# A one-element exponential ahead of the first exponential that follows each run of Gelus

## The chip, the cores and the metric

The kernel runs on one core of a Trainium2 chip. The metric is device time in microseconds of one execution, lower is better; several executions are timed and the median counts. The engines of the core are TensorE (PE, with its weight loads as PEld), VectorE (DVE), ScalarE (ACT), GpSimd (POOL) and SyncE (SP, which issues transfers). Each engine works through its own instructions in order and waits on semaphores for the others.

## The reference

Two layers, each an attention with a compressive memory and then a GeGLU feed-forward, on 2048 tokens of width 512 in bfloat16. The attention works on four segments of 512 tokens, 32 heads of 16.

```python
def _A_ref(x, wq, wk, wv, wo, beta):
    ...
    for s in range(N):
        ...
        logits = jnp.einsum('bhqd,bhkd->bhqk', qs, ks) * scale + mask
        p = _softmax(logits, axis=-1)
        a_dot = jnp.einsum('bhqk,bhkd->bhqd', p, vs)
        pq = phi(qs)
        num = jnp.einsum('bhld,bhde->bhle', pq, M)
        ...
        pk = phi(ks)
        M = M + jnp.einsum('bhld,bhle->bhde', pk, vs)
        z = z + jnp.einsum('bhld->bhd', pk)
    ...

def _B_ref(x, w_gate, w_up, w_down):
    return _gelu(x @ w_gate) * (x @ w_up) @ w_down

x = A_x
x = x + _A_ref(_layernorm(x, axis=-1), A_wq, A_wk, A_wv, A_wo, A_beta)
x = x + _B_ref(_layernorm(x, axis=-1), B_w_gate, B_w_up, B_w_down)
x = x + _A_ref(_layernorm(x, axis=-1), A_wq, A_wk, A_wv, A_wo, A_beta)
x = x + _B_ref(_layernorm(x, axis=-1), B_w_gate, B_w_up, B_w_down)
```

Here phi(t) is t + 1 for positive t and exp(t) elsewhere. So ACT computes two kinds of function that matter below: Exp (softmax and phi) and Gelu (feed-forward).

## The kernel before

The whole input, all weights and the activations stay on the chip. The work is cut into eight attention blocks (two layers by four segments, numbered k = 0 to 7) and eight feed-forward blocks of the same numbering. A block of scores (token S) fills four of the eight PSUM banks, each of 128 x 512 float32, and an exponential (tokens e for half of them, E for all four) reads them, scales, and writes bfloat16 into a slot of the tile pt. The next block of scores that uses the same banks has to wait until the exponentials have read them. Masks on POOL (or DVE), products with the values on PE, and transposes on DVE follow.

A feed-forward block computes 14 tiles of gate (G) and up (P) products. The gate either is copied to gel_sb first and gets its Gelu there (copy g, then l), or its Gelu is taken straight from PSUM (L). DVE then multiplies by the up product (p). All Gelus of a block stand together on ACT, so that its instructions go from Exp to Gelu and back.

What sets the order is one long string of tokens, ORDER, written out by hand: a loop in `run` reads token by token and emits the instructions of each, and each engine keeps that order. A token's first letters choose the routine, a letter v, s or g behind them the engine (DVE, ACT, POOL), and numbers the block, tile, bank and so on. The attention of later segments is interleaved with the feed-forward of earlier ones, so scores of the next block come right behind the Gelus.

ACT can hold the table of Exp or that of Gelu. The build puts an ACT_TABLE_LOAD ahead of each activation that needs the other one; the load carries line numbers of that activation, and takes over waits that were the activation's. Copies on ACT (ACT.Copy) bring no load with them. There are 14 loads in all: one at the start, seven to Gelu (line 753) and six back to Exp: five ahead of an exponential of scores (line 598, in `exponential`) and one ahead of an exponential for phi (line 655, in `phi_exp`). After the last two feed-forward blocks no exponential follows.

The lines that the prediction names: 481 and 483 are the two forms of a dense product on PE (in four column groups, or whole), 593 the scores, 631 the products with the values, 608 the mask on POOL, 638 a transpose on DVE of those products, 753 the Gelu, 819 the multiplication by the up product, 490 and 492 copies out of PSUM on ACT and DVE, 496 layer-norm statistics, 742 a memset of `constant_column`, 454 and 455 two small exponentials of beta at the start.

Of the kernel before, what the change touches and what calls it, by code (L numbers as in the profile page):

```python
# [9 lines left out]
ACT = mybir.ActivationFunctionType  # L10
ALU = mybir.AluOpType
ENG = mybir.EngineType
F32 = mybir.dt.float32
# [9 lines left out]
L = 512  # L23
# [271 lines left out]
def run(nc, cst, seg, wrk, psp, A_x, A_wq, A_wk, A_wv, A_wo, A_beta, B_x, B_w_gate, B_w_up, B_w_down, out):  # L295
# [86 lines left out]
    def vaug(k):  # L382
        return vaugs[(k - 1) % SETS if k else SETS]
# [90 lines left out]
    def ps(*name):  # L474
        return ps_all[:, bank[name], :]
# [81 lines left out]
    def dense(code, k, b, h, n, bk, columns):  # L557
        name = (code, k, b, h)
        if name not in done:
            done[name], bank[name] = 0, bk  # L560
        pairs, group = ops_of(code, k, b, h)
        for _ in range(n):
            i = done[name]
            done[name] += 1
            size = group or len(pairs)
            if group:
                dst = ps(*name)[:, half * (i // group):half * (i // group) + half]
            elif code == "W":
                c0, c1 = down_columns(h)
                dst = ps(*name)[:, 0:c1 - c0]  # L570
            else:
                dst = ps(*name)
            l, r = pairs[i]
            product(dst, l(), r(), columns, i % size == 0, i % size == size - 1)
# [5 lines left out]
    def score(k, v, b0, b1, s):  # L580
        a_q, a_kf, a_kx = q[k], kf[k], kx[k]
        banks = (b0, b0 + 1, b1, b1 + 1)
        slot[k, v] = s
        bank["S", k, v] = (b0, b1)
        for r in range(2):
            for b, par, ki, q0, n, c0 in ROUNDS_OF[2 * v + r][0]:
                for j in range(4):
                    rows = slice(32 * j, 32 * j + 32 if 1 in par else 32 * j + 16)
                    if 1 in par:
                        lhsT = a_kx[rows, b, ki, 0:P] if 0 in par else a_kx[rows, b, ki, C:3 * C]  # L590
                    else:
                        lhsT = a_kf[rows, b, P * ki:P * ki + P]
                    multiply(ps_all[:, banks[j], UNIT * r + c0:UNIT * r + c0 + n], lhsT=lhsT, rhs=a_q[rows, b, q0:q0 + n],  # L593
                             start=True, stop=True, tile_position=(32 * j, 0))

    def exponential(k, v, p, n):
        s, b0 = slot[k, v], bank["S", k, v][p]
        nc.scalar.activation(out=pt_all[:, s:s + 2, 2 * p:2 * p + 2 * n, :].rearrange("p r h c -> p h r c"),  # L598
                             in_=ps_all[:, b0:b0 + 2 * n, :].rearrange("p h (r c) -> p h r c", r=2), func=ACT.Exp, scale=SCALE)
# [19 lines left out]
    def values(k, u, bk):  # L619
        b, par = u // 2, u % 2  # L620
        bank["F", k, u] = bk
        work = []
        for i in range(*USED[par]):
            t = ROUNDS * b + i
            for _, par2, ki, q0, n, o in ROUNDS_OF[t][0]:
                work.append((t, vz if len(par2) > 1 else vaug(k), ki, q0, n, o))
        work.sort(key=lambda w: w[1] is vz)
        for m, (t, va, ki, q0, n, o) in enumerate(work):
            for j in range(4):
                g = (DH + 1) * (par * H // 2 + 4 * b + j)  # L630
                multiply(ps("F", k, u)[32 * j:32 * j + 32, q0:q0 + n], lhsT=va[:, ki * VW + g:ki * VW + g + 32],  # L631
                         rhs=pt_all[:, slot_of(k, t), j, o:o + n], start=(m == 0), stop=(m == len(work) - 1),
                         tile_position=(0, 32 * j))
# [115 lines left out]
            load(part(vz, slice(C * a, C * a + C), a), part(vaug(k), slice(0, C), a))  # L749


    def gelu(dst, src):
        nc.scalar.activation(out=dst, in_=src, func=ACT.Gelu_apprx_tanh)  # L753

# [7 lines left out]
    def turn_tile(m, j, n, bk):  # L762
        name = ("T", m, j)
        if name not in done:
            done[name], bank[name] = 0, bk
        for _ in range(n):
            kt = done[name]
            done[name] += 1
            turn_by_pe(turned(name)[:, kt, :], xn_of[m, j][:, kt * P:(kt + 1) * P], ident[:])  # L769
# [7 lines left out]

    engine = {"v": nc.vector, "s": nc.scalar, "g": nc.gpsimd}

    for token in ORDER:  # L780
        code, *arg = token.split("/")
        eng = engine.get(arg[0])
        if eng is not None:
            arg = arg[1:]
        i = [int(a) for a in arg]
        k, b = (i + [0, 0])[:2]
        if code in ("Q", "K", "V", "O", "G", "P", "QH", "KH", "GH", "W"):
            dense(code, *i)
        elif code == "S":
            score(*i)  # L790
        elif code == "F":
            values(*i)
        elif code in ("D", "N", "U"):
            memory_product(code, *i)
        elif code == "T":
            turn_tile(*i)
        elif code == "e":
            exponential(k, b, i[2], 1)
        elif code == "E":
            exponential(k, b, 0, 2)  # L800
        elif code == "M":
            mask(eng, k, b)
        elif code in ("q", "k"):
            copy(eng, set_of(k)["qk".index(code)][:, b, :], ps(code.upper(), k, b, 0))
        elif code in ("qh", "kh"):
            cols = slice(half * i[2], half * i[2] + half)
            copy(eng, set_of(k)["qk".index(code[0])][:, b:b + 2, cols], folded((code.upper(), k, b, i[2])))
        elif code == "v":
            copy(eng, by_head(vaug(k))[:, b, :, :, 0:DH], ps("V", k, b, 0).rearrange("p (h a e) -> p h a e", a=2, e=DH))
        elif code == "g":  # L810
            copy(eng, gel_sb[:, b, :], ps("G", k, b, 0))
        elif code == "gh":
            copy(eng, gel_sb[:, 2 * b:2 * b + 2, half * i[2]:half * i[2] + half], folded(("GH", k, b, i[2])))
        elif code == "l":
            gelu(gel_sb[:, b, :], gel_sb[:, b, :])
        elif code == "L":
            gelu(gel_sb[:, b, :], ps("G", k, b, 0))
        elif code == "p":
            nc.vector.tensor_tensor(out=gel_sb[:, b, :], in0=gel_sb[:, b, :], in1=ps("P", k, b, 0), op=ALU.mult)  # L819
        elif code == "w":  # L820
            c0, c1 = down_columns(i[2])
            add_to_x(k, b, c0, c1, ps("W", k, b, i[2])[:, 0:c1 - c0])
        elif code == "o":
            add_to_x(k, b, 0, D, ps("O", k, b, 0))
        elif code == "s":
            c0, c1 = down_columns(i[2])
            load(of[:, tile_of(k) + b, c0:c1], x_sb[:, tile_of(k) + b, c0:c1])
        elif code == "m":
            masked(eng, k, b)
        elif code == "z":  # L830
            values_shared(k)
        elif code == "f":
            value_turn(k, b)
        elif code == "r":
            value_scale(k, b)
        elif code == "b":
            value_back(k, b)
        elif code == "a":
            add_up(eng, k, b)
        elif code == "x":  # L840
            phi_exp(*i)
        elif code == "n":
            e = e_of[i[0], i[1], i[2]]
            eng.tensor_scalar(out=e[:], in0=e[:], scalar1=1.0, scalar2=None, op0=ALU.min)  # L844
        elif code == "y":
            phi_sum(*i)
        elif code == "t":
            phi_turn(k, b)
        elif code == "d":
            inverse(k)  # L850
        elif code == "am":
            scaled(*i)
        elif code == "tm":
            scaled_turn(k, b)
        elif code == "ua":
            add_sums(k)
        elif code == "ub":
            spread(k)
        elif code == "st":
            stats(k, b)  # L860
        elif code == "sc":
            scales(k, b)
        elif code == "xn":
            xn_of[k, b] = normed(eng, k, b, i[2])
        elif code == "xt":
            nc.sync.dma_start_transpose(out=part_of_x(k, b), in_=xn_of[k, b][:])
        elif code == "tc":
            copy(eng, part_of_x(k, b), turned(("T", k, b)))
        elif code == "c":
            constant_column(k)  # L870
        elif code == "X":
            load_x(k)
        elif code == "Zo":
            load(w_att["o"][:, k, :], w_view(A_wo)[:, k, :])
        elif code == "Zg":
            ffn_columns(wg_sb, B_w_gate, k)
        elif code == "Zu":
            ffn_columns(wu_sb, B_w_up, k)
        else:
            down_rows(slice(2 * k, 2 * k + 2))  # L880
# [55 lines left out]
```

## Time and profile before

| what | value |
|---|---|
| median of the runs | 540.68 us (540.21, 540.68 and 1830.87) |
| profiled execution, own time | 542.1 us |
| its span in the profile | 540.2 us |
| ACT busy | 423.3 us (78%), 503 instructions |
| DVE busy | 442.1 us (82%) |
| POOL busy | 275.6 us (51%) |
| granted clock of TensorE | full in all 40 slices of the span |

The span runs from the first to the last instruction that the profile holds, and the rest of an execution's time lies around it. Busy time of PE is given in the prediction; matmuls overlap in its pipeline, so the ends of matmuls are modelled. A row of the timeline gives start, duration, engine, line, operation, operands, how many instructions are merged, and, in brackets, the idle time of that engine ahead of the row and who ended it.

### The profile page before, as it was taken

Reading aid. Unit: us, or ns where it says so; the run is one execution under the profiler, and the core shown is the slowest. Engines: PE = TensorE matmul, PEld = TensorE weight load, DVE = VectorE, ACT = ScalarE, POOL = GpSimd, SP = SyncE. Lnnn points to the kernel's source line nnn. Section 1 sums busy time; section 2 is a strip of 40 time slices with the busy share of each in tenths; the row PEclk is TensorE's granted clock in tenths of the full one; section 3 lists DMA queues with packets and bytes.
Section 4 is the critical chain, followed back from the end, with each engine's and each line's share of the span. In section 5 each row is a group of like instructions: output and inputs, shape, how many; then the busy total and the mean of one; then the engine's idle time right before and its main releaser. Section 6 shows DMA issues by size and latency. Waiting matters only on the chain.

```text
span 540.2 us, 21100 instructions
## 1 busy us (share of the span) xinstructions
PE 521.6 (97%) x9255; PEld 276.9 (51%) x9321; DVE 442.1 (82%) x864; ACT 423.3 (78%) x503; POOL 275.6 (51%) x356
## 2 busy tenths in 40 slices
PE   7989999999999999999999999999999999999997
PEld 4444467455654455544554444454555456545444
DVE  7988998899899988899887888978888886776543
ACT  6989998998999778887889888887799867830430
POOL 4798764267658787578752545641544036501000
PEclk9999999999999999999999999999999999999999
DMA  8594143213002133230432130312031005200001
GB/s 276 132 183 88 36 74 124 60 32 65 9 16 46 24 61 46 39 42 11 63 51 54 29 51 4 62 24 30 4 81 24 2 2 81 63 1 0 21 0 59
DMA packets 69134, 27.98 MB, mean 52 GB/s; under 512 B 53426, under 2 KB 69042, under 8 KB 69042
## 3 DMA queue, kind: packets, MB, share of 16 engines
q1 hardware_dynamic: 68752, 26.36, 24.1%
q8 instruction: 73, 1.20, 0.9%
q10 hardware_dynamic: 290, 0.26, 0.2%
q14 instruction: 19, 0.16, 0.1%
HBM read 9.70 MB, written 2.10 MB: 22 GB/s over the span
## 4 chain that ended last, share of the span: by engine, by line
PE 86%; DMA 4%; ACT 3%; issue 2%; DVE 2%; SPq 1%; POOL 0%; ACTq 0%; DVEq 0%
PE ps L483 46%; PE ps L481 24%; PE ps L593 8%; PE ps L631 6%; ACT pt L598 2%; DMA x_sb<-in_A_x_dram 2%; DMA xnT<-xn 2%; PE ps L698 1%; SPq L312 1%; DMA wg_sb<-in_B_w_gate_dram 1%; POOL pt L608 0%; DVE byq L638 0%; ACT wd_sb L490 0%; PE ps L769 0%; DVE st L496 0%
## 5 line engine op out<-in xcount | busy, mean ns | idle before, releaser
L598 ACT ACTIVATE pt<-ps 128x1024 bf16<-128x1024 f32 (+1 forms) x231 | 275.3, 1234 | 47.1 <-PE ps L593 33.7
L608 POOL TENSOR_SCALAR_AFFINE_SELECT pt<-pt 128x256 bf16<-128x256 bf16 (+1 forms) x192 | 106.3, 571 | 158.0 <-ACT pt L598 152.1
L819 DVE TENSOR_TENSOR gel_sb<-gel_sb,ps 128x512 bf16<-128x512 bf16 x112 | 72.3, 680 | 22.4 <-PE ps L483 15.4
L483 PE MATMUL ps<-wd_sb,gel_sb 128*128 128x512 bf16 (+1 forms) x335 | 71.6, 351 | 2.2 <-issue 1.9
L483 PE MATMUL ps<-xnT,wu_sb 128*128 128x512 bf16 x279 | 67.4, 379 | 0.9 <-issue 0.5
L483 PE MATMUL ps<-xnT,wg_sb 128*128 128x512 bf16 (+1 forms) x292 | 60.4, 344 | 1.2 <-issue 1.0
L757 DVE TENSOR_TENSOR x_sb<-x_sb,ps 128x512 bf16<-128x512 bf16 (+1 forms) x68 | 43.4, 649 | 19.3 <-PE ps L483 13.1
L638 DVE STREAM_TRANSPOSE byq<-ps 128x512 f32<-128x512 f32 x64 | 45.4, 709 | 10.9 <-PE ps L631 8.4
L481 PE MATMUL ps<-xnT,wg_sb 128*32 128x512 bf16 (+1 forms) x800 | 50.1, 373 | 0.0
L492 DVE CAST gel_sb<-ps 128x512 bf16<-128x512 f32 x61 | 40.9, 679 | 10.3 <-PE ps L483 7.3
L753 ACT ACTIVATE gel_sb<-gel_sb 128x512 bf16<-128x512 bf16 x85 | 47.4, 623 | 0.6 <-DVE gel_sb L492 0.5
L483 PEld LDWEIGHTS <-gel_sb 128*128 128x128 bf16 x353 | 32.2, 98 | 29.7 <-issue 1.5
L753 ACT ACTIVATE gel_sb<-ps 128x512 bf16<-128x512 f32 x27 | 15.7, 592 | 36.5 <-PE ps L483 35.1
L483 PEld LDWEIGHTS <-wu_sb 128*128 128x128 bf16 x288 | 27.5, 98 | 32.2 <-issue 0.4
L496 DVE BATCH_NORM_STATS2 st<-x_sb 128x6 f32<-128x512 bf16 x60 | 40.7, 678 | 0.5 <-DMA x_sb<-in_A_x_dram 0.2
L481 PE MATMUL ps<-xnT,wu_sb 128*32 128x512 bf16 x640 | 39.8, 379 | 0.6 <-ACT pt L598 0.6
L483 PEld LDWEIGHTS <-wg_sb 128*128 128x128 bf16 x304 | 27.8, 98 | 23.7 <-issue 2.0
L678 POOL TENSOR_SCALAR kx<-kf,masks 128x256 bf16<-128x256 bf16 (+1 forms) x30 | 38.6, 1299 | 0.9 <-PE ps L593 0.7
L616 POOL TENSOR_SCALAR_AFFINE_SELECT pt<-pt 64x1024 bf16<-64x1024 bf16 x26 | 31.0, 1191 | 12.6 <-ACT pt L598 11.7
L844 POOL TENSOR_SCALAR e<-e 128x512 bf16<-128x512 bf16 x21 | 31.7, 1512 | 6.9 <-ACT e L655 6.3
L631 PE MATMUL ps<-pt,vaug 128*32 128x256 bf16 (+2 forms) x1344 | 34.8, 238 | 0.2 <-POOL pt L608 0.2
L481 PE MATMUL ps<-wd_sb,gel_sb 128*32 128x512 bf16 (+1 forms) x604 | 34.8, 364 | 0.0
(138 smaller groups left out, 863.6 us busy)
## 6 DMA issues: line engine op xcount, KB each, us to landing
vz<-vaug SPq DMA_DIRECT2D x14, 136.0 KB, 2.6
wu_sb<-in_B_w_up_dram SPq DMA_DIRECT2D x8, 224.0 KB, 3.9
wg_sb<-in_B_w_gate_dram SPq DMA_DIRECT2D x8, 224.0 KB, 3.8
wd_sb<-in_B_w_down_dram SPq DMA_DIRECT2D x7, 256.0 KB, 4.7
x_sb<-in_A_x_dram SPq DMA_DIRECT2D x3, 512.0 KB, 7.2
out_dram<-x_sb SPq DMA_DIRECT2D x12, 128.0 KB, 1.8
xnT<-xn SPq DMA_TRANSPOSE x48, 2.6
wk_sb<-in_A_wk_dram SPq DMA_DIRECT2D x2, 256.0 KB, 4.5
```

What stands on the lines that cost most here:

```text
L481: multiply(dst[r], lhsT=lhsT[:, r], rhs=rhs, start=start, stop=stop, tile_position=(0, 32 * c))
L483: multiply(dst, lhsT=lhsT, rhs=rhs, start=start, stop=stop)
L492: eng.tensor_copy(out=dst, in_=src)
L496: nc.vector.bn_stats(out=st[:, 0, :], in_=x_sb[:, tile_of(m) + j, :])
L593: multiply(ps_all[:, banks[j], UNIT * r + c0:UNIT * r + c0 + n], lhsT=lhsT, rhs=a_q[rows, b, q0:q0 + n], start=True, stop=True, tile_posit ...
L598: nc.scalar.activation(out=pt_all[:, s:s + 2, 2 * p:2 * p + 2 * n, :].rearrange("p r h c -> p h r c"), in_=ps_all[:, b0:b0 + 2 * n, :].rea ...
L608: nc.gpsimd.affine_select(out=view, in_=view, pattern=[[0, 4], [0, n], [1, C]], compare_op=ALU.is_ge, fill=0.0, base=C, channel_multiplier=-1)
L631: multiply(ps("F", k, u)[32 * j:32 * j + 32, q0:q0 + n], lhsT=va[:, ki * VW + g:ki * VW + g + 32], rhs=pt_all[:, slot_of(k, t), j, o:o + n ...
L638: nc.vector.transpose(out=byq[k, u // 2][:, u % 2, :, :].rearrange("p a c -> p (a c)"), in_=ps("F", k, u))
L753: nc.scalar.activation(out=dst, in_=src, func=ACT.Gelu_apprx_tanh)
L757: nc.vector.tensor_tensor(out=xt, in0=xt, in1=src, op=ALU.add)
L819: nc.vector.tensor_tensor(out=gel_sb[:, b, :], in0=gel_sb[:, b, :], in1=ps("P", k, b, 0), op=ALU.mult)
```

## The change

A tile of two float32 on one partition is set to zero by DVE, ahead of the loop over the tokens. Whenever the loop comes to a token of an exponential (e or E for scores, x for phi) for the first time since a Gelu, it first emits an Exp on ACT of one element of that tile into the other. This happens six times. Nothing reads the result.

```diff
+    idle = cst.tile([1, 2], F32, name="idle")
+    nc.vector.memset(idle[:], 0.0)
+
+    def exponentials_next():
+        nc.scalar.activation(out=idle[:, 1:2], in_=idle[:, 0:1], func=ACT.Exp)
+
     def gelu(dst, src):
         nc.scalar.activation(out=dst, in_=src, func=ACT.Gelu_apprx_tanh)
...
+    gelus = False
     for token in ORDER:
         code, *arg = token.split("/")
+        if gelus and code in ("e", "E", "x"):
+            exponentials_next()
+            gelus = False
+        gelus = gelus or code in ("l", "L")
         eng = engine.get(arg[0])
```

How the instructions stand on ACT at the third of the six places (Gelus of feed-forward block 2, then the scores of attention block 4). gel_sb holds gates, ps is PSUM, pt the exponentials of scores, e an exponential for phi; the names in brackets are the semaphores waited for. Before:

```order
L753 ACTIVATE gel_sb<-ps 128x512
L753 ACTIVATE gel_sb<-gel_sb 128x512 x7
L598 ACT_TABLE_LOAD [waits DVE_49,PE_49]
L598 ACTIVATE pt<-ps 128x2x2x256 [waits Pool_49]
L655 ACTIVATE e<-q 128x512 [waits DMAHW7_49,DMAHW0_49]
L598 ACTIVATE pt<-ps 128x2x2x256 [waits PE_49]
```

And the same place with the change:

```order
L759 ACTIVATE gel_sb<-ps 128x512
L759 ACTIVATE gel_sb<-gel_sb 128x512 x7
L756 ACT_TABLE_LOAD
L756 ACTIVATE idle<-idle 1x1
L598 ACTIVATE pt<-ps 128x2x2x256 [waits DVE_49,PE_49,Pool_49]
L655 ACTIVATE e<-q 128x512 [waits DMAHW7_49,DMAHW0_49]
```

The load now belongs to the new instruction and carries no wait; the waits for DVE and PE went to the exponential. The fifth and sixth places (blocks 4 and 5) read alike. At the first place (block 0) the load of before waited for DVE alone:

```order
-L598 ACT_TABLE_LOAD [waits DVE_49]
-L598 ACTIVATE pt<-ps 128x2x2x256 [waits PE_49] x2
+L759 ACT_TABLE_LOAD
+L759 ACTIVATE gel_sb<-gel_sb 128x512 [waits Activation_49]
+L759 ACTIVATE gel_sb<-gel_sb 128x512 [waits DVE_49]
+L759 ACTIVATE gel_sb<-gel_sb 128x512 x12
+L756 ACT_TABLE_LOAD
+L756 ACTIVATE idle<-idle 1x1
+L598 ACTIVATE pt<-ps 128x2x2x256 [waits DVE_49,PE_49]
+L598 ACTIVATE pt<-ps 128x2x2x256 [waits PE_49]
```

Here too the wait for DVE went over to the exponential; the rows of Gelus only have new line numbers. At the second place the load stood ahead of an exponential for phi and had no wait before either. On DVE one memset of the new tile is added ahead of the first statistics of the token list; PE, POOL and SP keep their instructions and their order.

## The prediction

> **What bounds the kernel now.** I read the busy shares first, then the waits of TensorE (PE), then the groups of ScalarE (ACT), then the stretch of the timeline around each switch of ACT's table from Gelu back to Exp. The page's first part, busy time and share of the span:
>
> ```profile
> PE 521.6 (97%) x9255; PEld 276.9 (51%) x9321; DVE 442.1 (82%) x864; ACT 423.3 (78%) x503; POOL 275.6 (51%) x356
> ```
>
> PE is the bound: 521.6 of 540.2 us, so 18.6 us of idleness is all that a change off PE can take away. What PE waits for, from the table of waits of PE (waiter, awaited, us in total, times, longest):
>
> ```profile
> PE ps L483 <- DMA xnT<-xn: 2.2, 2, 1.3
> PE ps L593 <- ACT pt L598: 1.7, 3, 0.9
> PE ps L481 <- ACT pt L598: 0.6, 1, 0.6
> ```
>
> PE waits for exponentials of scores (line 598) 2.3 us in these two rows, three times and once. The question is whether those four waits lie behind table switches. The groups of ACT (busy us, mean ns, then idle us before them and who ended it):
>
> ```profile
> L598 ACT ACT_TABLE_LOAD x5 | 6.4, 1283 | 5.5 <-PE ps L593 3.7 <-issue 1.3 <-DVE gel_sb L819 0.5
> L655 ACT ACT_TABLE_LOAD x1 | 1.3, 1283 | 0.0
> ```
>
> There are six switches back to Exp, five carried by an exponential of scores and one by an exponential of q. Each load takes 1.283 us, and ACT sat idle 5.5 us ahead of the five: 3.7 for scores of PE, 1.3 listed as issue, 0.5 for VectorE (DVE). In these cases the load stood behind a wait that concerns only the exponential.
>
> Now the six places in the timeline (start us, duration us, engine, line, operation; in brackets the idle time ahead and who ended it). Third switch:
>
> ```profile
> 235.46 0.62 ACT L753 ACTIVATE gel_sb<-gel_sb 128x512 bf16<-128x512 bf16 x1
> 237.85 0.64 PE L593 MATMUL ps<-q,kf 16*128 16x256 bf16 x12
> 238.54 1.28 ACT L598 ACT_TABLE_LOAD   x1 [2.46 <-PE ps L593]
> 239.83 1.02 ACT L598 ACTIVATE pt<-ps 128x1024 bf16<-128x1024 f32 x1
> 240.91 1.69 PE L481 MATMUL ps<-xnT,wu_sb 128*32 128x512 bf16 x28 [0.58 <-ACT pt L598]
> ```
>
> The last Gelu ends at 235.46 + 0.62 = 236.08. ACT then idles 2.46 us until the scores are there, loads 1.28 us, and only then runs the exponential. PE stands still for 0.58 us at 240.33, until that exponential has emptied its banks. Fifth switch:
>
> ```profile
> 369.70 0.60 ACT L753 ACTIVATE gel_sb<-ps 128x512 bf16<-128x512 f32 x1 [0.45 <-PE ps L481]
> 371.09 0.41 PE L593 MATMUL ps<-q,kx 32*128 32x64 bf16 x20
> 371.56 1.28 ACT L598 ACT_TABLE_LOAD   x1 [1.27 <-PE ps L593]
> 372.86 1.94 ACT L598 ACTIVATE pt<-ps 128x1024 bf16<-128x1024 f32 x2
> 373.93 0.20 PE L593 MATMUL ps<-q,kx 32*128 32x64 bf16 x2 [0.17 <-ACT pt L598]
> 374.85 0.40 PE L593 MATMUL ps<-q,kx 32*128 32x64 bf16 x10 [0.71 <-ACT pt L598]
> ```
>
> Gelu ends at 370.30, the scores come 1.27 us later, the load delays both exponentials, and the next scores, which go into the same banks, wait 0.17 + 0.71 = 0.88 us. Sixth switch:
>
> ```profile
> 424.73 2.18 ACT L753 ACTIVATE gel_sb<-gel_sb 128x512 bf16<-128x512 bf16 x4
> 427.70 0.40 PE L593 MATMUL ps<-q,kx 32*128 32x64 bf16 x12
> 428.19 1.28 ACT L598 ACT_TABLE_LOAD   x1 [1.27 <-issue]
> 429.48 1.94 ACT L598 ACTIVATE pt<-ps 128x1024 bf16<-128x1024 f32 x2
> 431.47 0.29 PE L593 MATMUL ps<-q,kx 32*128 32x64 bf16 x8 [0.86 <-ACT pt L598]
> ```
>
> Gelu ends at 426.91 and the load begins at 428.19. The bracket says issue, but by the program's order this load waits for DVE and PE, and the scores end at 427.70 + 0.40 = 428.10, so I read it as the wait for scores. PE then waits 0.86 us. The stalls sum to 0.58 + 0.88 + 0.86 = 2.32 us, the whole 1.7 + 0.6 of the table above: every such wait of PE lies right behind a load.
>
> The other three switches have no stall of PE. First (ahead of it, Gelus without a gap), second and fourth:
>
> ```profile
> 101.88 1.28 ACT L598 ACT_TABLE_LOAD   x1
> 103.17 1.94 ACT L598 ACTIVATE pt<-ps 128x1024 bf16<-128x1024 f32 x2
> 106.11 1.94 ACT L598 ACTIVATE pt<-ps 128x1024 bf16<-128x1024 f32 x2 [0.48 <-POOL pt L608]
> 108.36 0.29 PE L593 MATMUL ps<-q,kf 16*128 16x64 bf16 x8
> ```
>
> ```profile
> 170.81 1.28 ACT L655 ACT_TABLE_LOAD   x1
> 172.64 1.86 ACT L598 ACTIVATE pt<-ps 128x2048 bf16<-128x2048 f32 x1
> 175.69 0.40 PE L593 MATMUL ps<-q,kf 16*128 16x256 bf16 x12
> ```
>
> ```profile
> 294.67 0.60 ACT L490 ACTIVATE kf<-ps 128x512 bf16<-128x512 f32 x1 [0.33 <-PE ps L483]
> 295.72 1.28 ACT L598 ACT_TABLE_LOAD   x1 [0.45 <-DVE gel_sb L819]
> 297.16 1.94 ACT L598 ACTIVATE pt<-ps 128x1024 bf16<-128x1024 f32 x2 [0.15 <-PE ps L593]
> 299.54 0.40 PE L593 MATMUL ps<-q,kf 16*128 16x256 bf16 x12
> ```
>
> At the first two the load starts as soon as ACT is free, so there is nothing to pull forward. At the fourth ACT is free at 295.27 and waits 0.45 us for DVE, yet the exponential waits another 0.15 us for its scores after the load: this load is hidden already. PE has some room behind each. The scores at 108.36 follow the exponentials that end at 108.05 (0.31 us), those at 175.69 the one that ends at 174.50 (1.19), those at 299.54 the ones that end at 299.10 (0.44).
>
> **The change, part by part.** It adds one memset on DVE, six Exp of one element on ACT, and moves six loads from the exponential to the new instruction, which waits for nothing. The other engines issue the same rows in the same order.
>
> The memset stands ahead of the first statistics of the token list. The nearest rows are that statistic and a memset of 8 columns:
>
> ```profile
> 10.59 0.69 DVE L496 BATCH_NORM_STATS2 st<-x_sb 128x6 f32<-128x512 bf16 x1 [0.21 <-DMA x_sb<-in_A_x_dram]
> ...
> 14.15 0.07 DVE L742 MEMSET gel_sb<- 128x8 uint32 x1
> ```
>
> DVE idles 0.21 us there for a transfer of x, so 0.07 us is covered. Without that cover DVE would be 0.07 us late.
>
> The one-element Exp has no row. The nearest is the Exp of 32 elements, the farthest one of 512:
>
> ```profile
> L455 ACT ACTIVATE tmp_e<-ps 128x32 f32<-128x32 f32 x1 | 0.2, 217 | 0.0
> L655 ACT ACTIVATE e<-q 128x512 bf16<-128x512 bf16 x24 | 14.6, 629 | 0.0
> ```
>
> I take 0.21 us, by the row of 32 elements: from 32 to 512 elements it grows by 0.41 us, under 1 ns an element, so 1 element saves almost nothing on it. The ends for the range are 0 (it overlaps the next ACTIVATE wholly) and 0.63.
>
> At the first two switches and the fourth: two of them get 0.21 us later on ACT (0.31 and 1.19 us of room behind them, so PE sees nothing; with 0.63 the first would cost 0.32). At the fourth the load could start at 295.27, the new Exp ends at 295.27 + 1.28 + 0.21 = 296.76, and the scores still decide at 297.16. Nothing gained, nothing lost.
>
> Third switch: the load starts at 236.08, the Exp ends at 237.57, ahead of the scores at 238.54. The exponential starts 1.29 us earlier (239.83 less 238.54), so PE's 0.58 us go. Fifth: load to 371.58, Exp to 371.79. The scores are there at 371.56, so 0.23 us of load and Exp still stick out, and the exponentials start at 371.79 instead of 372.86, 1.07 us earlier: more than the 0.88 us stall. Sixth: 426.91 + 1.28 + 0.21 = 428.40 instead of 429.48, 1.08 us earlier against a stall of 0.86. What decides behind each is then PE's own row of work.
>
> Sum: 0.58 + 0.88 + 0.86 = 2.3 us less. With 0.63 for the new Exp, the fifth and sixth give 0.65 each and the first loses 0.32: 1.6 us less. If the pulled-forward exponentials carried through whole, 1.29 + 1.07 + 1.08 = 3.4 us is the most. The profiled execution took 542.1 us for a span of 540.2, 1.9 outside it; it becomes 539.8. It lies 1.4 us over the median of the runs, 540.68, and I take the difference off that: 540.7 - 2.3 = 538.4.
>
> Here the Trainium skill speaks against the change: ScalarE: Activation LUTs, section What ACT_TABLE_LOAD costs, prices a switch at about 1.28 us of load and 1.38 us of drain, 2.66 us together. This trace has the load's 1.283 us but no drain around it: at the first switch the exponential starts at 103.17, 0.01 us after the load. By the page, with 1.38 us more at each moved switch, the fifth and sixth would come 0.3 us later than now, and the sum would be about 2.2 us more, not 2.3 less. The trace does not bear that out, as far as it shows switches without a wait.
>
> **The rivals.** First, the gain is given back: PE gets there earlier and meets the next thing that isn't ready. For it speaks the longest thing besides PE's own work on the chain that ended last, after the third switch (start us, us, what):
>
> ```profile
> 340.48 0.72 DVE byq L638
> 343.25 4.20 DMA xnT<-xn
> ```
>
> If that chain did not move, the third switch's 0.58 us would be lost there: 1.74 left, 538.9. Against it: the chain starts from products of PE (DVE's transpose reads what PE wrote), so it moves too, and the fifth and sixth switches come later, with no transfer on the chain after 347.5. If all is absorbed, 540.7, no change.
>
> Second, the change doesn't do what it says: the load stays behind a wait, or the exponential waits longest for something else (its third wait, for POOL, that the load did not carry). Then 540.7. Against it: in the new order the load and the Exp carry no wait, and the exponentials after the third, fifth and sixth loads start 0.01 to 0.02 us after the load ends, so POOL was not late by then; whether it was in time 1.1 us earlier these rows do not show.
>
> Third, on the other side: the switch is not over when the load is over, and the new Exp pays for the rest. Its place is ACT between load and first exponential; call its time D. The third switch gains its 0.58 up to D = 1.88; the fifth and sixth gain 1.28 - D each, at most their stalls; the first loses what D exceeds 0.31, the second 1.19, the fourth 1.04 (0.60 of slack ahead of its scores and 0.44 behind). The sum turns at D = 1.1 us. Were D another load's time on top, 1.28 + 0.21 = 1.49, it is -0.58 + 0.42 + 1.18 + 0.30 + 0.45 = 1.8 us more: 542.5. Against it: no row of ACT under 512 elements without a load takes over 0.6 us. Of this kind is the drain of the Trainium skill's page above, and it would give 540.7 + 2.2 = 542.9.
>
> **How the numbers follow.** The sum at work: 0.62, 538.4, by itself 537.3 (3.4 us) to 539.1 (1.6 us). Gain given back in part or whole, 538.9 to 540.7: 0.20. No effect, 540.7: 0.11. Slower by the switch's rest, 542.5: 0.07. Of these, 0.03 go to the rule of the Trainium skill's page on ScalarE, at 542.9. The runs shown differ by 0.5 us (540.21 and 540.68; 1830.87 I leave out as a disturbance), and the profiled one is 1.4 over. So the range goes 0.5 below the most that can be gained, 536.8, and 0.3 above no effect, 541.0; the slower rival and part of the scatter, under 0.2, stay outside. A difference of 2%, 10.8 us, is about what a measurement of this kernel can tell from no change. PE's waits for exponentials are 2.3 us, the one rival that loses loses 2; so within 2% has 0.98, and 0.01 goes to either side for what I haven't seen.
>
> **What would show it.** In the profile of the changed kernel: six loads and six one-element Exp on the new line, of 1.28 and 0.2 us; idle time ahead of the loads gone (5.5 us now) and found ahead of the exponentials, waiting for PE; the three stalls of PE behind the third, fifth and sixth switches gone or under 0.2 us; no new wait of PE at 106 to 109. I am wrong if the new Exp takes more than 0.63 us, if the stalls go and the span doesn't shrink by 1.5 us or more (then the first rival, and the place where PE waits instead must show), or if the exponentials after the loads start no earlier against their scores than before.

## The result, and the profile after

The changed kernel takes 538.0 us (median of 5 runs, 537.55 to 538.56), the kernel before 540.69 in the runs beside it: a ratio of 0.9949, with an interval of 0.9933 to 0.9964. That is 2.7 us less. The profiled execution took 538.0 us for a span of 535.9; the one before had 542.1 and 540.2, so the two profiles differ by 4.1 to 4.3 us, more than the medians; the second run of the kernel before shows below where most of that rest lies. Two executions far outside the others, one of 1830.87 us of the kernel before and one of 666.4 us of the Copy kernel below, are in no ratio.

PE in the first part of the page after (busy us, share of the span, instructions):

```profile
PE 520.5 (97%) x9255; PEld 276.5 (52%) x9321; DVE 441.4 (82%) x865; ACT 424.1 (79%) x509; POOL 275.9 (51%) x356
```

Of the 4.3 us by which the span is shorter, 3.2 are idleness of PE (18.6 us before, 15.4 now). The other 1.1 us are busy time, which rests on modelled ends. The groups of ACT that belong to the new line (busy us, mean ns, then idle us before them):

```profile
L756 ACT ACT_TABLE_LOAD x6 | 7.7, 1283 | 0.1
L756 ACT ACTIVATE idle<-idle 1x1 f32<-1x1 f32 x6 | 1.2, 202 | 0.1
```

All six loads moved to the new line and cost 1.283 us each as before, but ACT idles 0.1 us ahead of them instead of 5.5. The Exp of one element takes 0.202 us. The waits of PE after:

```profile
PE ps L483 <- DMA xnT<-xn: 1.4, 2, 1.0
PE ps L483 <- ACT pt L598: 0.2, 1, 0.2
```

The rows for scores (line 593, 1.7 us) and column-group products (line 481, 0.6 us) that waited for exponentials are gone. Of the waits for exponentials only the 0.2 us at line 483, which were there before, are left. The timeline of the third switch after:

```profile
235.00 1.28 ACT L756 ACT_TABLE_LOAD   x1
236.29 0.20 ACT L756 ACTIVATE idle<-idle 1x1 f32<-1x1 f32 x1
236.76 0.63 PE L593 MATMUL ps<-q,kf 16*128 16x256 bf16 x12
237.45 1.02 ACT L598 ACTIVATE pt<-ps 128x1024 bf16<-128x1024 f32 x1 [0.96 <-PE ps L593]
239.06 1.68 PE L481 MATMUL ps<-xnT,wu_sb 128*32 128x512 bf16 x28
240.67 0.40 PE L593 MATMUL ps<-q,kf 16*128 16x256 bf16 x12
```

Load and Exp stand in the time in which ACT waits anyway; 0.96 us of the wait are left, and they stand ahead of the exponential now. PE's products at 239.06 have no bracket, where they had 0.58 us. Fifth and sixth:

```profile
367.72 0.60 ACT L759 ACTIVATE gel_sb<-ps 128x512 bf16<-128x512 f32 x1 [0.45 <-PE ps L481]
368.34 1.28 ACT L756 ACT_TABLE_LOAD   x1
369.12 0.41 PE L593 MATMUL ps<-q,kx 32*128 32x64 bf16 x20
369.63 0.20 ACT L756 ACTIVATE idle<-idle 1x1 f32<-1x1 f32 x1
369.74 1.90 ACT L598 ACTIVATE pt<-ps 128x1024 bf16<-128x1024 f32 x2
371.72 0.40 PE L593 MATMUL ps<-q,kx 32*128 32x64 bf16 x12
374.54 0.29 PE L593 MATMUL ps<-q,kx 32*128 32x64 bf16 x8
...
423.62 1.28 ACT L756 ACT_TABLE_LOAD   x1
424.40 0.40 PE L593 MATMUL ps<-q,kx 32*128 32x64 bf16 x12
424.73 2.58 PE L481 MATMUL ps<-xnT,wu_sb 128*32 128x512 bf16 x44
425.03 1.90 ACT L598 ACTIVATE pt<-ps 128x1024 bf16<-128x1024 f32 x2
427.24 0.29 PE L593 MATMUL ps<-q,kx 32*128 32x64 bf16 x8
```

At the fifth the scores end at 369.12 + 0.41 = 369.53 and the exponentials start at 369.74, since a piece of load and Exp sticks out. That is early enough: the next scores at 371.72 run in one piece of 12 and without a bracket, where they came in two pieces with 0.17 and 0.71 us of waiting.

To compare kernels without the scatter of whole executions, I use a distance on PE: from the scores that the first exponential after a switch reads to a later block of scores (the next one at the third and sixth switch, the next but one at the fifth). Before it is 242.53 - 237.85 = 4.68 us at the third switch, 377.67 - 371.09 = 6.58 at the fifth and 431.47 - 427.70 = 3.77 at the sixth. After it is 3.91, 5.42 and 2.84. The three switches give 0.77 + 1.16 + 0.93 = 2.86 us. A further 0.11 us goes just behind the third switch, where two products on PE start 0.33 us apart before (243.96 and 244.29) and 0.22 after (242.09 and 242.31), so PE gains about 2.97 us in all. This second step repeats in the other runs with one Exp at that switch and is in none without; no bracket names what PE waits for there.

### The profile page after: what moved, and what is told of

It reads as the page before. It is cut to its first block, busy times and chain, and to the rows that moved or that the text cites. A ratio compares the mean times of both kernels' runs of the same rounds, so it can differ in the third digit from the quotient of the medians.

```text
span 535.9 us, 21107 instructions
## 1 busy us (share of the span) xinstructions
PE 520.5 (97%) x9255; PEld 276.5 (52%) x9321; DVE 441.4 (82%) x865; ACT 424.1 (79%) x509; POOL 275.9 (51%) x356
## 4 chain that ended last, share of the span: by engine, by line
PE 93%; DMA 2%; DVE 2%; issue 1%; ACT 1%; POOL 1%; DVEq 0%; SPq 0%
PE ps L483 50%; PE ps L481 26%; PE ps L593 9%; PE ps L631 7%; DMA xnT<-xn 1%; ACT pt L598 1%; PE ps L698 1%; DMA x_sb<-in_A_x_dram 1%; POOL pt L608 0%; DVE st L402 0%; PE ps L775 0%; DVE byq L638 0%; PE ps L447 0%; DVE xn L391 0%; DVE gel_sb L492 0%
## 5 line engine op out<-in xcount | busy, mean ns | idle before, releaser
L830 DVE TENSOR_TENSOR gel_sb<-gel_sb,ps 128x512 bf16<-128x512 bf16 x112 | 72.2, 679 | 20.3 <-PE ps L483 15.4
```

## The experiments

The theory that I tested (A): the gain is PE's stall behind three of the six loads, and it is as large as the time by which the exponentials come earlier, up to that stall. Its rivals: B, the gain comes from elsewhere (the other three switches, or the memset and the tiles shifted by the new one), and C, it only matters that the load stands ahead of the wait, whatever time the extra instruction takes.

### The three switches with a stall, and the other three

A counter of the switches picks those at which the Exp is emitted.

```diff
-    gelus = False
+    gelus, switch = False, 0
...
         if gelus and code in ("e", "E", "x"):
-            exponentials_next()
+            switch += 1
+            if switch in (3, 5, 6):
+                exponentials_next()
             gelus = False
```

> The one-element Exp at the third, fifth and sixth switch alone. Theory A (the gain is PE's stall behind these three loads, 0.77 + 1.15 + 0.93 = 2.85 us by PE's rows of the two profiles): the whole gain of the change, about 538.0 us, ratio 0.995; on PE, from the scores at a switch to the next scores 3.91 us at the third (4.68 before), from the scores to the next but one at the fifth 5.42 (6.58 before), to the next at the sixth 2.84 (3.77 before). Theory B (the gain comes from the other places, or from the shifted tiles and the memset): part of it or nothing, up to 540.7, and the first 90 us shorter by 0.8 in every variant that has the memset.

Measured: 537.33 us beside 540.52, ratio 0.9932 (0.9915 to 0.9949); distances 3.91, 5.43 and 2.85 us. The whole gain is there: 2.84 us by the distances, and 3.2 by the medians. The other kernel has `(1, 2, 4)` in place of `(3, 5, 6)`.

> The one-element Exp at the first, second and fourth switch alone. Theory A: no gain, 540.7 us, at most 0.2 more, with the three stalls of PE as before (4.68, 6.58 and 3.77 us between the scores). Theory B: a part of the gain stays, 538.0 to 540.0.

Measured: 540.28 us beside 540.52, ratio 0.9990 (0.9979 to 1.0001); distances 4.67, 6.58 and 3.77 us. No gain that can be told from none, and all three stalls are back, at the same size as in the kernel before (its timeline at the third, fifth and sixth switch):

```profile
237.65 1.28 ACT L598 ACT_TABLE_LOAD   x1 [2.46 <-PE ps L593]
240.02 1.69 PE L481 MATMUL ps<-xnT,wu_sb 128*32 128x512 bf16 x28 [0.58 <-ACT pt L598]
...
374.15 0.40 PE L593 MATMUL ps<-q,kx 32*128 32x64 bf16 x10 [0.71 <-ACT pt L598]
...
430.64 0.29 PE L593 MATMUL ps<-q,kx 32*128 32x64 bf16 x8 [0.85 <-ACT pt L598]
```

So the gain sits at the third, fifth and sixth switch, and the other three Exps give nothing.

### An instruction that moves no table

```diff
-        nc.scalar.activation(out=idle[:, 1:2], in_=idle[:, 0:1], func=ACT.Exp)
+        nc.scalar.activation(out=idle[:, 1:2], in_=idle[:, 0:1], func=ACT.Copy)
```

> A one-element Copy in place of the one-element Exp, at all six places: the same memset, tile and number of instructions on ACT, but the load stays with the exponential and its waits. Theory A: no gain, 540.7 us, up to 0.3 more where the Copy has no wait to hide in. Theory B (placement, memset): 538.0.

Measured: 539.87 us beside 540.52, ratio 0.9984 (0.9972 to 0.9996). The loads stay at lines 598 and 655. At the third switch the Copy runs at once, and the load waits behind it for the scores:

```profile
234.03 0.18 ACT L756 ACTIVATE idle<-idle 1x1 f32<-1x1 f32 x1
236.58 1.28 ACT L598 ACT_TABLE_LOAD   x1 [2.37 <-PE ps L593]
```

The distances are those of before: 4.67, 6.57 and 3.77 us. So the three stalls are all there, and the theory holds where it speaks. The time is 0.65 us lower than before all the same, and the interval just leaves out no change. The profile puts no part of that at the switches: at the sixth switch this execution stands 2.30 us ahead of the kernel before, of which 1.41 had come by the scores at 38 us and 0.53 between 203 and 236 us. The next two runs bear on that.

### The kernel before once more, and the memset alone

> The kernel before, unchanged, once more. It shows how far two executions of one program differ, and where. The first stretch is the question: at the scores near 38 us the four variants profiled so far, all with the memset, stand 0.6 to 1.7 us earlier than the kernel before. Theory A (scatter of the first transfers): this profile, too, differs there from the first one by up to 1.5 us, and its time is 540.5, ratio 1.000. Theory B (the memset or the shifted tiles make the start earlier): the start stays where it was, within 0.2 us.

Measured: 540.73 us beside 540.70, ratio 0.9998 (0.9990 to 1.0007). Its profile stands 1.14 us ahead of the first profile of the same program at the scores near 38 us, 0.76 at 237.85 and 0.68 at the sixth switch. The rows of PE at the place where they part, in the first profile (two rows) and in this one:

```profile
38.07 0.39 PE L483 MATMUL ps<-xnT,wk_sb 128*128 128x512 bf16 x1 [1.29 <-DMA xnT<-xn]
38.39 0.40 PE L593 MATMUL ps<-wd_sb 16*128 16x256 bf16 x12
```

```profile
37.25 0.40 PE L593 MATMUL ps<-wd_sb 16*128 16x256 bf16 x12
```

In the first profile PE waited 1.29 us for a transposing transfer of the normalised input; here the wait is not there, and in the first profile of the changed kernel it is 0.38 us. That profile stands 4.23 us ahead of the first profile of before at the scores behind the sixth switch. Of these, 2.86 came at the three switches, 0.81 by the scores near 38 us, 0.28 between 203 and 236 us, where the unchanged kernel lost 0.39 on itself, and the rest in smaller steps. So most of what the profiled pair differ by beyond the switches lies in stretches in which one program differs from itself by as much.

The memset alone leaves out the lines in the token loop and keeps the tile:

```diff
-    gelus = False
     for token in ORDER:
         code, *arg = token.split("/")
-        if gelus and code in ("e", "E", "x"):
-            exponentials_next()
-            gelus = False
-        gelus = gelus or code in ("l", "L")
```

> The tile and its memset alone, with no Exp ahead of any exponential. Theory A: as the kernel before, 540.5 us, stalls of PE of 4.68, 6.58 and 3.77 us between the scores. Theory B (part of the gain is the tile and the memset): 539.7 or less, the start 0.6 us or more earlier than in the kernel before.

Measured: 540.54 us beside 540.70, ratio 0.9996 (0.9986 to 1.0007); distances 4.66, 6.58 and 3.77 us. Its start stands 0.94 us ahead of the first profile, less than that of the unchanged kernel, so the start says nothing about the memset. Rival B falls. What the 0.65 us of the Copy kernel are stays open: tile and memset don't give them, the switches don't, and the start scatters by more than that. The medians of the kernels with Exps at some of the switches are also 0.2 to 0.4 us lower against 540.52 than their distances give, so the Copy need not be the cause; no run separates this.

### A longer instruction behind the load

The tile gets 448 columns of bfloat16, and the Exp runs over all of them.

```diff
-    idle = cst.tile([1, 2], F32, name="idle")
+    idle = cst.tile([1, 448], BF16, name="idle")
...
-        nc.scalar.activation(out=idle[:, 1:2], in_=idle[:, 0:1], func=ACT.Exp)
+        nc.scalar.activation(out=idle[:], in_=idle[:], func=ACT.Exp, scale=0.0)
```

> An Exp of 448 elements in bfloat16 (about 0.56 us, 0.47 of it ahead of the next exponential) in place of one element, at all six places. Theory A, with the gain as long as the time that the exponentials come earlier, up to the stall: third switch 0.77, fifth and sixth 1.28 - 0.47 = 0.81 each, the first loses 0.47 - 0.27 = 0.20: 2.2 us less than before, 538.5; next scores at the fifth and sixth 0.35 and 0.12 us later than with one element. Rival C (it only matters that the load stands ahead of the wait): as the change, 538.0, with the same times between scores.

Measured: 537.77 us beside 540.52, ratio 0.9939 (0.9921 to 0.9957). The time alone speaks for C: its 538.0 is a ratio of 0.995 and lies in the interval, while A's 2.2 us less would be 0.9959, just outside. The distances speak for A: 3.90 us at the third, 5.77 at the fifth and 2.95 at the sixth, so 0.35 and 0.11 more than with one element, against 0.35 and 0.12 expected. At the first switch the scores come 3.81 us after those of the switch, 0.23 more than before (3.58), against 0.20 expected. The fifth switch of this kernel:

```profile
367.58 0.41 PE L593 MATMUL ps<-q,kx 32*128 32x64 bf16 x20
368.10 0.58 ACT L756 ACTIVATE idle<-idle 1x448 bf16<-1x448 bf16 x1
368.58 1.90 ACT L598 ACTIVATE pt<-ps 128x1024 bf16<-128x1024 f32 x2
370.19 0.74 PE L593 MATMUL ps<-q,kx 32*128 32x64 bf16 x12
373.35 0.29 PE L593 MATMUL ps<-q,kx 32*128 32x64 bf16 x8
```

The Exp takes 0.58 us and the exponentials follow 0.48 us after its start. The 12 scores at 370.19 need 0.74 us where 0.40 do without a wait: a part of PE's stall has come back. By the distances this kernel gains 0.78 + 0.81 + 0.82 - 0.23 = 2.2 us, and by the medians 2.75; the half microsecond between them is not at the switches and stays as open as that of the Copy kernel. So this run alone does not decide between A and C.

Then three such Exps behind each other (against the kernel with one of them):

```diff
-        nc.scalar.activation(out=idle[:], in_=idle[:], func=ACT.Exp, scale=0.0)
+        for _ in range(3):
+            nc.scalar.activation(out=idle[:], in_=idle[:], func=ACT.Exp, scale=0.0)
```

> Three Exps of 448 elements one behind the other at all six places, about 1.7 us ahead of the next exponential. Theory A: the third switch still gains its 0.77 us (2.46 us of wait less 1.28 less 0.39); the fifth and sixth lose 1.7 - 1.28 = 0.4 each, the first 1.4, the second 0.5, the fourth 0.7: 2.6 us more than before, 543.1. Rival C (it only matters that the load stands ahead of the wait): 538.0.

Measured: 543.41 us beside 540.70, ratio 1.0046 (1.0031 to 1.0062), 2.7 us slower, where A had 2.6 and C a gain. Its first, second and fourth switch:

```profile
101.73 1.79 ACT L757 ACTIVATE idle<-idle 1x448 bf16<-1x448 bf16 x3
103.43 1.90 ACT L598 ACTIVATE pt<-ps 128x1024 bf16<-128x1024 f32 x2
104.48 1.24 PE L483 MATMUL ps<-xnT,wu_sb 128*128 128x512 bf16 x5 [1.29 <-ACT pt L598]
...
174.32 1.85 ACT L598 ACTIVATE pt<-ps 128x2048 bf16<-128x2048 f32 x1
176.22 0.40 PE L593 MATMUL ps<-q,kf 16*128 16x256 bf16 x12 [0.46 <-ACT pt L598]
...
300.10 0.40 PE L593 MATMUL ps<-q,kf 16*128 16x256 bf16 x10 [0.41 <-ACT pt L598]
```

The three take 1.79 us, and the next exponential comes 1.70 us after their start. PE, which had room behind these switches, now waits 1.29, 0.46 and 0.41 us for exponentials. Place by place, against the kernel before, PE is 1.45 us later at the first, 0.52 at the second, 0.73 at the fourth, 0.40 at the fifth and 0.40 at the sixth, and still 0.78 earlier at the third: 2.7 us in sum, the whole of what was measured. Expected were 1.4, 0.5, 0.7, 0.4, 0.4 and -0.77. Rival C falls.

### The change once more

> The change as it is, once more, on the chip of the other runs of this call. Theory A: 537.9 us, ratio 0.995, and between the scores the 3.91, 5.42 and 2.84 us of its first profile; beside the kernel with three of the six Exps it shows whether those at the first, second and fourth switch cost anything (0 to 0.1 us expected).

Measured: 537.60 us beside 540.70, ratio 0.9940 (0.9925 to 0.9954), with distances of 3.91, 5.42 and 2.84 us, the same as the first time to 0.01. Against the kernel with three of the six Exps (0.9932, 0.9915 to 0.9949) the intervals overlap. As far as these runs can tell three Exps are as good as six, and no version is shown to be better than the change.

## Why the prediction was right

**The place of the gain.** The prediction said that every wait of PE for exponentials in two rows of its table lay behind the third, fifth and sixth load, and that these would go. They went, and the kernel with only these three Exps has the whole gain. This step is shown, not only argued.

**The size.** 538.4 us was forecast and 538.0 measured, 2.3 and 2.7 us less. The interval of the ratio goes from 1.9 to 3.6 us less, so the times alone do not tell the two apart; the distances do. The term that was too small is the stalls, read from the brackets as 0.58, 0.88 and 0.86 us. By the distances they are 0.77, 1.16 and 0.93, 2.86 in sum. A row of PE ends later than the next one can start, as two rows of the kernel before show, ahead of the third stall:

```profile
238.42 1.05 PE L481 MATMUL ps<-xnT,wu_sb 128*32 128x512 bf16 x16
239.29 1.04 PE L481 MATMUL ps<-wv_sb,xnT 128*32 128x512 bf16 x16
```

The groups of 16 start 0.87 us apart, but a group lasts 1.05. A bracket counts from the end of the row before, so it leaves out the overlap that the stall destroyed. At the third switch, from the group at 239.29 to the one behind the stall at 240.91 are 1.62 us; without a stall 0.87; the stall is 0.75, not 0.58. At the sixth the products at 424.73 of the kernel after end at 427.31 and the scores start at 427.24, so 0.07 us go on top of the bracket's 0.86. At the fifth the same overlap is 0.06 (products from 369.68 to 371.78, scores at 371.72). There the stall also cut a group of 12 scores in two; about 0.2 us of the 1.16 are left for that, which is not shown by itself.

At the fifth switch the exponentials come 1.15 us earlier against their scores (1.77 us before, 0.62 after), and the scores behind them come 1.16 earlier: there the gain is all that the earlier exponentials bring, and hardly any room is left. The longer Exp shows the same, since its 0.37 us more cost 0.35 there.

**The room at the other switches.** The prediction had 0.31, 1.19 and 1.04 us at the first, second and fourth switch. The three long Exps, 1.70 us, cost 1.45, 0.52 and 0.73 us, so the room was 0.25, 1.18 and 0.97. At the first switch the place was wrong and the near number is luck: the prediction read the room at the scores at 108.36, behind the second pair of exponentials, but in the kernel with the long Exps PE waits at 104.48, at a product, while the first pair (103.43 to 105.33) still runs.

**The cost of the new Exp.** 0.21 us were taken, 0.202 measured. The next exponential starts 0.11 us after it has begun (369.63 to 369.74), so only about half of its time lies on the path. No stall appeared at the first, second and fourth switch, as forecast: at the first the next scores come 3.58 us after those of the switch, before and after.

**The rivals.** That the gain is given back at the transposing transfers near 347 us did not happen beyond scatter: from before these transfers to after them the changed kernel loses 0.14 us on the first profile of before and gains 0.05 in its second profile, while the unchanged kernel differs from itself there by 0.27. That the exponentials wait longest for POOL did not happen: at the fifth and sixth switch they start right behind the Exp, at the third with the scores. The rival on the other side, a time D between load and exponential that turns the sum at about 1.1 us, had the right dependence on D but too large a D: with one element D is 0.11 us, with 448 it is 0.48 and the sum is still a gain, with three times 448 it is 1.70 and the kernel is 2.7 us slower. The prediction's own terms give 2.8 us more for a D of 1.70.

**The drain.** At the fifth switch the Gelu ends at 367.72 + 0.60 = 368.32, the load starts at 368.34 and ends at 369.62, the Exp starts at 369.63 and the exponential at 369.74. The Trainium skill, ScalarE: Activation LUTs, section What ACT_TABLE_LOAD costs, adds 1.38 us of drain to a load of 1.28. The load agrees, and the drain does not show on either side of it. By an estimate from that figure of the Trainium skill a drain behind the load would have made D about 1.5 us, and the long Exps show what a D of 1.70 does.

## What to carry to other kernels

Where an engine needs a set-up ahead of an instruction, look at whose waits the set-up carries. If it stands behind a wait that concerns only the data, a tiny instruction of the same kind without that wait pulls it into the idle time, and here this paid where the bound engine waits for the result, at three of six places. How much it pays is the smaller of the stall and the time won, and it turns into a loss as soon as the extra instruction outlasts the wait and the room behind it. Measure such effects of a few tenths of a per cent on the distance between two landmarks in the profile, which repeats to 0.02 us here while the executions of one kernel scatter by 1 to 3 us.

## What the runs showed of the hardware that I had not expected

The bracket ahead of a row of PE understates a stall, by 0.07 to 0.28 us each here, since a row of PE without a wait starts before the row ahead of it ends by the profile: by 0.18 us for a group of 16 products (0.87 between starts, 1.05 of length), by 0.06 and 0.07 for the scores at the fifth and sixth switch. An Exp of one element costs ACT 0.202 us, but the next ACTIVATE starts 0.11 us after it began, so only about half of it delays what follows; for 448 elements it is 0.48 of 0.58 us. The first 38 us of one and the same program differed by 1.14 us between two executions, by one transfer that PE did or didn't have to wait for.
